# Retention steps of 192 tokens, made a burst early, and one PSUM bank for the second product

## The chip, the cores and the metric

The kernel runs on one core of one Trainium2 chip. The metric is the device time of one execution in microseconds (us), the median of several runs. TensorE (PE in the profile) multiplies, with its weight loads listed as PEld; VectorE is DVE, ScalarE is ACT, GpSimd is POOL, SyncE is SP. An engine works through its own instructions in order, and waits on semaphores for the others.

## The reference

Eight batch entries of 576 tokens, eight heads of 64, go through a retention (an attention with a decay in place of a softmax). The result, 4608 tokens of 512 values, goes through a feed-forward layer with 2048 hidden values.

```python
scores = scale * np.matmul(q, k.transpose(0, 1, 3, 2))
gamma = 1.0 - 2.0 ** (-5.0 - np.arange(H))
Dmat = np.where(rel >= 0, gamma ** rel, 0.0)         # rel = row - column
attn = np.matmul(scores * Dmat, v)                   # then heads side by side: x [4608, 512]
h = x @ w_in                                         # [4608, 2048]
out = (h * (1.0 / (1.0 + np.exp(-1.702 * h)))) @ w_out
```

## The kernel before, in words

**The recorder.** Every operation is recorded with what it reads and writes (`Rec.op`), in the order of the code; the recorder puts it at the end of its engine's queue and adds the semaphore waits. So the order of each engine's work is written out by hand: the order of the calls.

**Retention.** The decay factors into a power on the query side (`gq`, applied when the output leaves PSUM) and one on the value side (`vfac`, applied to v in place by `scale_v`, on VectorE). What is left is a causal product. An entry is cut into five steps of 128, 128, 128, 128 and 64 tokens (`ROWS`); step n is entry n // 5, part n % 5. In a step, scores k q^T go to the bank pair `psS`, VectorE masks them into `sm` (`mask_s`, line 426), and the output is intra (v against the masked scores) plus carried (the state against q). The state, the sum of k^T v over the tokens before, is added up part by part in `zacc` and cast into `zq` (`evac_z`). From entry 1 on everything is made of 64x64 products, which use one quarter of the array each (`scores`, line 404; `values_quarters`, lines 445 intra, 457 state, 464 carried), and k and v of the upper four heads are loaded 64 rows shifted (`load_shifted`). `evac_o` (line 573) multiplies the output by `gq` into `xT`, a buffer for all 4608 tokens.

**Keys and queries turned.** Scores need q and k with the head dimension on partitions. Steps below 10 (`PE_TURNS`, entries 0 and 1) turn them on TensorE (`transposes`, line 366) and copy them with ScalarE (`evac_t`). Later steps use `dma_turn` (line 586): two DMA transposes on SyncE's queue, q of the step and k of the next tile, into one of four buffers `qk`. `burst(n)` asks for the turn of step n + 3.

**Bursts.** `burst(n)` (line 606) holds the products of step n - 1's output and state and, between the two halves of these, the scores of step n. Then VectorE masks step n, evicts step n - 1 and updates the state (`finish`). The second half waits for the first to end (`own=first`). When an entry's last step is finished, `load_entry` asks for the loads three entries on, on POOL's queue (three slots, `NST`).

**Feed-forward.** Nine chunks of 512 tokens. `hidden(c, f)` (line 634) makes 128 of the 2048 hidden values with four matmuls of 512 columns into `psH[0]` or `psH[1]`, and ScalarE writes the activation (line 639). `project(c, r, g)` (line 687) adds a quarter of the second product for 128 tokens, again four matmuls; after g = 3 the bank is copied to `osb` (line 699 VectorE, line 696 ScalarE) and stored by SyncE (line 702). Such a group of four matmuls is called a unit here. From chunk 1's projection on, row blocks alternate between `psU` and `psW` (`pair`).

**Order on TensorE.** Entry 0 alone, chunk 0's products with entry 1's steps between, `hidden_half` of chunk 1 (bursts 8, 9, 10 between), chunk 1's projection (bursts 11 to 13), `hidden` of chunk 2 (bursts 14 to 18), then `region(c)` for chunks 3 to 8. A region alternates the 16 units of chunk c - 1's projection with the 16 of chunk c's first product, in the order O H O H O O H H for each row block, and spreads the bursts that the next chunk needs over its 32 units. Chunk 8's projection ends the kernel.

Of the kernel before, what the change touches and what calls it, by code (L numbers as in the profile page):

```python
# [26 lines left out]
PE_TURNS = 10  # L27
QK_SCALE = 1.0 / math.sqrt(DH)

# [100 lines left out]
def bass_retnet_parallel__then__act_gelu_quick_kernel(  # L130
# [11 lines left out]
    with es:  # L142
# [8 lines left out]
        mask = sb("mask", [P, 2, P], FP32)  # L151
        posj = sb("posj", [P, NC], FP32)
# [9 lines left out]
        gq = sb("gq", [P, NC, HP, 128], FP32)  # L162
# [3 lines left out]
        qk = [sb(f"qk{i}", [P, 2, HP, 128], BF16) for i in range(NQK)]  # L166
        sm = [sb(f"sm{i}", [P, 2, HP, 128], BF16) for i in range(3)]
        zs = sb("zs", [P, HP, 128], BF16)
        xT = sb("xT", [P, HP, B * S], BF16)
# [7 lines left out]
        psS = ps("psS", [P, 2, HP, 128])  # L177
# [36 lines left out]
        def load_entry(b, first=0):  # L214
            if first == 0:
                load(b, 0, "k")
            for c in range(first, NC):
                load(b, c, "q")
                if c + 1 < NC:
                    load(b, c + 1, "k")  # L220
                load(b, c, "v")
# [18 lines left out]
        def constants_first():  # L240
# [22 lines left out]
            for hp in range(HP):  # L263
                R.op("ACT", lambda e, hp=hp: e.activation(
                    gq[:, 0, hp, :], posa.ap(), AF.Exp, scale=lng[:, hp : hp + 1]),
# [7 lines left out]
        def constants_shifted():  # L273
            for r in range(2):
# [3 lines left out]
                    r=["rel"], w=[("mask", 1)])  # L278
            R.op("DVE", lambda e: e.tensor_copy(vfac[1][:, 0:4, :], vfac[0][:, 0:4, :]),
# [14 lines left out]
        def regroup(what):  # L294
# [6 lines left out]
            if what == "gq":  # L301
                t = gT[1][0:64, 8:13, :].bitcast(FP32).rearrange("p c (u n) -> p c u n", u=2)
                swap(gq[0:64, :, 1:4:2, :], gq[64:128, :, 0:4:2, :], t,
# [8 lines left out]
        def later_gq(hp):  # L312
            R.op("ACT", lambda e: e.activation(
                gq[:, 1:NC, hp, :], posi.ap(), AF.Exp, scale=lng[:, hp : hp + 1]),
# [35 lines left out]
        def sides(n):  # L350
# [3 lines left out]
            for a, t, nm, m in ((0, st_q, "q", n), (1, st_k, "k", n if n < NC else n + 1)):  # L354
                if m < NSTEP:
# [15 lines left out]
        def evac_t(n):  # L371
            R.op("ACT", lambda e: e.activation(qk[n % NQK].ap(), psT, AF.Copy),  # L372
# [42 lines left out]
        def mask_s(n):  # L415
            b, c = divmod(n, NC)
            N = ROWS[c]
            if b == 0:
                m = mask[:, 0, 0:N].unsqueeze(1).to_broadcast([P, 2 * HP, N]) if c != 3 else mask3
                o = sm[n % 3].ap().rearrange("p a h c -> p (a h) c")[:, :, 0:N]  # L420
                i = psS.ap().rearrange("p a h c -> p (a h) c")[:, :, 0:N]
            else:
                m = mask[:, :, 0:N].unsqueeze(1).to_broadcast([P, 4, 2, N])
                o = sm[n % 3].ap().rearrange("p a (t u) c -> p (a t) u c", u=2)[:, :, :, 0:N]
                i = psS.ap().rearrange("p a (t u) c -> p (a t) u c", u=2)[:, :, :, 0:N]
# [3 lines left out]
        def values_quarters(n):  # L429
# [46 lines left out]
            if n + 1 < NSTEP:  # L476
                intra(n + 1)
            R.op("PE", part(1), r=r, ps=["O", "Z"], own=first)

# [87 lines left out]
        def evac_o(n, o=None):  # L567
# [3 lines left out]
            t0 = S * b + 128 * c  # L571
            if b > 0:
# [3 lines left out]
                    gq[:, c, :, 0:N].rearrange("p (u j) n -> p u j n", u=2), ALU.mult),  # L576
                    r=[("gq", min(c, 1))], w=[("xT", b, c)], ps=["O", "Z"])
# [381 lines left out]
```

## Time and profile before

| | us |
|---|---|
| three runs | 308.57, 307.38, 306.63 |
| their median | 307.38 |
| the profiled execution, its own time | 306.58 |
| its span, first to last instruction | 304.7 |
| TensorE busy, share of the span | 297.3, 98% |
| ScalarE, VectorE, POOL busy | 108.8, 147.8, 154.2 |
| first product: one matmul of 128x512, modelled | 0.379 |
| mask of 1024 columns (line 426) | 1.223 |
| activation of 512 columns (line 639) | 0.597 |

The profile is of one execution. Its time in the device's account is 1.9 us more than the span that the trace covers. Times inside the trace are counted from the span's start. A busy share is not a rate: matmuls overlap, and a new one of 512 columns starts every 0.216 us although each is shown as 0.379.

### The profile page before, as it was taken

The numbers are of one execution on the slowest core, as the hardware profiler recorded it, in microseconds if no ns is written. First come the engines' busy times: TensorE is split into PE (matmuls) and PEld (weight loads), VectorE is DVE, ScalarE is ACT, GpSimd is POOL, SyncE is SP. The second block draws the span as 40 slices with busy tenths as digits, with TensorE's granted clock in tenths as the row PEclk, the third lists the DMA queues.
The fourth block names the chain that finished last, engine by engine and source line by source line (L and its number), as shares of the span: only waits on it lengthen the run. The fifth ranks groups of instructions, "written<-read, shape, count | busy, mean of one in ns | idle before, by whom it ended". The sixth has DMA issues, their size and how long they took to land.

```text
span 304.7 us, 7234 instructions
## 1 busy us (share of the span) xinstructions
PE 297.3 (98%) x3175; PEld 151.0 (50%) x3175; DVE 147.8 (48%) x246; ACT 108.8 (36%) x183; POOL 154.2 (51%) x208
## 2 busy tenths in 40 slices
PE   7899999999999999999999999999999999999996
PEld 3454545885444444444444444444444444444444
DVE  6689837554767833545546433444364431100012
ACT  8666524661035423322333223323233333333300
POOL 8998999999999999999850000000000000000000
PEclk9999999999999999999999999999999999999999
DMA  9999999999999999999999933213231000001012
GB/s 69 152 195 196 176 168 200 155 145 129 158 194 175 132 156 164 169 161 173 174 169 163 133 84 95 58 38 86 71 80 37 34 37 34 34 37 66 37 54 86
DMA packets 154303, 35.61 MB, mean 117 GB/s; under 512 B 144928, under 2 KB 149792, under 8 KB 154272
## 3 DMA queue, kind: packets, MB, share of 16 engines
q0 software_dynamic: 118384, 18.36, 87.3%
q1 hardware_dynamic: 35888, 16.79, 29.3%
q8 instruction: 25, 0.41, 0.6%
q14 instruction: 6, 0.05, 0.1%
HBM read 36.70 MB, written 9.44 MB: 151 GB/s over the span
## 4 chain that ended last, share of the span: by engine, by line
PE 83%; POOL 9%; DMA 3%; DVE 3%; issue 1%; POOLq 0%
PE psH L634 31%; PE psU L687 18%; PE psW L687 16%; PE psV L445 4%; DMA st_k<-in_k_dram 3%; PE psH L687 3%; PE psH L671 3%; POOL st_k L211 2%; POOL st_q L198 2%; PE psS L404 2%; PE psU L671 1%; PE psV L464 1%; POOL st_k L198 1%; POOL st_v L198 1%; PE psV L457 1%; POOL st_v L211 1%
## 5 line engine op out<-in xcount | busy, mean ns | idle before, releaser
L639 ACT ACTIVATE gT<-psH 128x512 bf16<-128x512 f32 x121 | 72.2, 597 | 153.8 <-PE psH L634 153.8
L634 PE MATMUL psH<-xT,w_in_sb 128*128 128x512 bf16 x484 | 118.1, 379 | 0.0
L426 DVE TENSOR_TENSOR sm<-psS,mask 128x1024 bf16<-128x1024 f32 (+1 forms) x39 | 43.5, 1114 | 85.1 <-PE psS L404 80.8
L634 PEld LDWEIGHTS psH<-xT,w_in_sb 128*128 128x128 bf16 x484 | 45.8, 98 | 54.9 <-ACT gT L639 1.6
L211 POOL DMA_DIRECT2D st_k<-in_k_dram x70 | 69.2, 1250 | 1.6 <-PE psV L464 0.9
L211 POOL DMA_DIRECT2D st_v<-in_v_dram x70 | 68.1, 1240 | 0.0
L687 PE MATMUL psU<-w_out_sb,gT 128*128 128x512 bf16 x256 | 62.7, 379 | 0.0
L687 PE MATMUL psW<-w_out_sb,gT 128*128 128x512 bf16 x224 | 54.8, 379 | 0.0
L198 POOL DMA_DIRECT2D st_q<-in_q_dram x40 | 52.7, 1317 | 0.2 <-issue 0.2
L687 PEld LDWEIGHTS psU<-w_out_sb,gT 128*128 128x128 bf16 x256 | 24.2, 98 | 28.0
L687 PEld LDWEIGHTS psW<-w_out_sb,gT 128*128 128x128 bf16 x224 | 21.3, 98 | 25.0
L343 DVE TENSOR_TENSOR st_v<-st_v,vfac 128x512 bf16<-128x512 bf16 x37 | 25.2, 680 | 3.1 <-DMA st_v<-in_v_dram 3.1
L699 DVE COPY osb<-psU 128x512 f32<-128x512 f32 x15 | 10.3, 687 | 28.6 <-PE psU L687 28.6
L573 DVE TENSOR_TENSOR xT<-psV,gq 128x512 bf16<-128x512 f32 (+1 forms) x35 | 21.9, 627 | 4.2 <-PE psV L464 4.2
L699 DVE COPY osb<-psW 128x512 f32<-128x512 f32 x14 | 9.6, 689 | 21.7 <-PE psW L687 21.7
L687 PE MATMUL psH<-w_out_sb,gT 128*128 128x512 bf16 x80 | 18.7, 379 | 0.0
L445 PE MATMUL psV<-sm,st_v 64*64 64x64 bf16 (+1 forms) x504 | 17.5, 214 | 0.3
L445 PEld LDWEIGHTS psV<-sm,st_v 64*64 64x64 bf16 x504 | 9.1, 104 | 15.7 <-issue 12.1
L372 ACT ACTIVATE qk<-psW 128x1024 bf16<-128x1024 bf16 x10 | 10.2, 1023 | 9.2 <-PE psW L366 9.2
L457 PE MATMUL psV<-st_v,st_k 64*64 64x64 bf16 x448 | 13.0, 192 | 0.0
L464 PE MATMUL psV<-qk,zq 64*64 64x128 bf16 (+1 forms) x224 | 12.6, 215 | 0.1
L687 PEld LDWEIGHTS psH<-w_out_sb,gT 128*128 128x128 bf16 x80 | 7.6, 98 | 8.5
(108 smaller groups left out, 212.7 us busy)
## 6 DMA issues: line engine op xcount, KB each, us to landing
out_dram<-osb SPq DMA_DIRECT2D x35, 256.0 KB, 2.4
st_q<-in_q_dram POOLq DMA_DIRECT2D x32, 128.0 KB, 17.5
st_k<-in_k_dram POOLq DMA_DIRECT2D x57, 64.0 KB, 17.2
st_v<-in_v_dram POOLq DMA_DIRECT2D x57, 64.0 KB, 17.2
w_out_sb<-in_moe_w_out_dram POOLq DMA_DIRECT2D x4, 512.0 KB, 11.9
w_in_sb<-in_moe_w_in_dram POOLq DMA_DIRECT2D x3, 512.0 KB, 7.8
st_k<-in_k_dram POOLq DMA_DIRECT2D x4, 128.0 KB, 4.2
st_v<-in_v_dram POOLq DMA_DIRECT2D x4, 128.0 KB, 4.6
```

The lines of the kernel that those rows point to most:

```text
L198: R.op("POOL", lambda e, d=d, s=s: e.dma_start(d, s), w=[(nm, sl, c)], dma=(nm, sl, c))
L211: R.op("POOL", lambda e: [e.dma_start(d, s) for d, s in parts], w=[(nm, sl, c)], dma=(nm, sl, c), parts=2)
L343: R.op(eng, lambda e: e.tensor_tensor(t, t, f, ALU.mult), r=[("vfac", min(b, 1))], w=[("v", sl, c)])
L426: R.op("DVE", lambda e: e.tensor_tensor(o, i, m, ALU.mult), r=[("mask", 0), ("mask", 1)] if b else mask3_keys if c == 3 else [("mask", 0)] ...
L445: i = e.matmul(psV[half(t), u, 128 * j + 64 * last : 128 * j + N], st_v[rows, sl, cc, 64 * h : 64 * h + 64], s[rows, j, 2 * t + u, 64 * la ...
L457: i = e.matmul(psV[half(j), u, 256 + 64 * t : 320 + 64 * t], st_k[rows, sl, cc, hs], st_v[rows, sl, cc, hs], start=False, stop=False, skip ...
L464: i = e.matmul(psV[half(t), u, 128 * j : 128 * j + N], zq[(c - 1) % 2][half(j), 2 * u + t, :], qk[n % NQK][half(j), 0, 2 * u + t, 0:N], st ...
L573: R.op("DVE", lambda e: e.tensor_tensor(xT[:, :, t0 : t0 + N].rearrange("p (u j) n -> p u j n", u=2), psV[:, :, 0:256].rearrange("p u (j n ...
L634: i = e.matmul(bank.ap(), w_in_sb[:, a, 128 * f : 128 * f + 128], xT[:, a, 512 * c : 512 * c + 512], start=(a == 0), stop=(a == 3))
L639: R.op("ACT", lambda e: e.activation(gT[c % 2][:, f, :], bank.ap(), AF.Gelu_apprx_sigmoid), w=[("gT", c % 2, f)], ps=[key])
L687: i = e.matmul(bank, gT[c % 2][:, f, 128 * r : 128 * r + 128], w_out_sb[:, f, :], start=(f == 0), stop=(f == NF - 1))
L699: R.op("DVE", lambda e: e.tensor_copy(osb[m].ap(), bank), w=[("osb", m)], ps=[key])
```

## The change

From entry 2 on an entry is done in three steps of 192 tokens, each of three 64-token blocks (`WIDE`, `NB`); step s is entry s // 3, part s % 3, so they run from 6 to 23. Every block has its own state ahead of it, so scores are only needed within a block (64 by 64, mask `mask64`). `prepare(s)` makes the scores of step s and the state products of its blocks, `states(s)` adds those up on VectorE in `zf` and casts them into `zw`, and both are called in the burst of step s - 1. `wide_burst(s)` holds the outputs of step s in two parts, with `prepare(s + 1)` between. The lists of products are interleaved so that four in a row use four quarters (`quads`). `dma_turn(s)` turns whole tiles of 128 tokens of both k and q into a buffer for two entries, and `wide_burst(s)` calls it for step s + 2. State products use `psW`, so the second product of the regions keeps to `psU` and is copied by ScalarE. `xT` becomes a ring of 1536 columns. The loads of entries 2 on are asked for in another order. Entries 0 and 1 keep their steps.

```diff
-PE_TURNS = 10
+XR = 1536
+WIDE = 192
+NB = WIDE // 64
+FIRST_WIDE = 6
+LAST_WIDE = B * S // WIDE - 1
...
+            if b >= 2:
+                for c, what in ((0, "kq"), (1, "kq"), (0, "v"), (1, "v"), (2, "kq"), (3, "k"),
+                                (2, "v"), (3, "v"), (3, "q"), (4, "kqv")):
+                    for one in what:
+                        load(b, c, one)
+                return
...
+                R.op("DVE", lambda e, rows=rows: e.tensor_copy(mask64[rows, :], mask[rows, 0, rows]),
...
-                if m < NSTEP:
+                if m < 2 * NC:
...
+        def tiles(s):
+            return ((0, 1), (2, 3), (4,))[s % NB]
+        def q_tiles(s):
+            return [("qT", s // NB % 2, m) for m in ((0, 1), (1, 2), (3, 4))[s % NB]]
+        def k_tiles(s):
+            return [("kT", s // NB % 2, m) for m in ((0, 1), (1, 2, 3), (3, 4))[s % NB]]
...
+        def dma_turn(s):
...
+            for m in tiles(s):
+                for a, t, nm in ((1, st_k, "k"), (0, st_q, "q")):
+                    rows = P if nm == "k" else ROWS[m]
+                    R.op("SP", lambda e, a=a, t=t, rows=rows, m=m: e.dma_start_transpose(
+                        out=qkT[:, buf, a, :, 128 * m : 128 * m + rows], in_=t[0:rows, sl, m, :]),
+                        r=[(nm, sl, m)], w=[(nm + "T", buf, m)] + olds, dma=("turn", buf, a, m))
...
+        def outputs(s, part):
+            c = s % NB
+            out = {}
+            for r in range(2):
+                u = (r + c + part) % 2
+                for t in range(2):
+                    todo = []
+                    for m in ((0, 2), (1,))[part]:
...
+                        for j in range(2):
+                            h = 4 * u + 2 * t + j
+                            todo.append((psV[half(t), u, WIDE * j + 64 * m : WIDE * j + 64 * m + 64],
+                                         st_v[half(r), sl, slot, 64 * h : 64 * h + 64],
+                                         smw[s % 2][half(r), j, 64 * (2 * m + t) : 64 * (2 * m + t) + 64],
+                                         adds if todo or part else starts))
+                    for m in range(1 if c == 0 else 0, NB):
+                        i = NB * c + m
+                        todo.append((psV[half(t), u, WIDE * r + 64 * m : WIDE * r + 64 * m + 64],
+                                     zw[half(r), s % 2, m, 2 * u + t, :],
+                                     qkT[half(r), s // NB % 2, 0, 2 * u + t, 64 * i : 64 * i + 64],
+                                     adds))
+                    out[r, t] = todo
+            return out
...
+        def prepare(s, turn):
+            c = s % NB
+            kv = kv_keys(s, "k") + kv_keys(s, "v")
+            done = R.op("PE", products(quads(joined(state_part(s, 1, 0, turn),
+                                                    state_part(s, 1, 1, turn)))),
+                        r=kv, ps=["O", "Z", "W"])
+            todo = [state_part(s, 0, 0, turn), state_part(s, 0, 1, turn), wide_scores(s)]
+            if c < 2:
+                todo.insert(0, state_part(s, 2, 0, turn))
+            R.op("PE", products(quads(joined(*todo))),
+                 r=kv + q_tiles(s) + k_tiles(s), ps=["S", "W"])
+            R.op("DVE", lambda e: e.tensor_tensor(
...
+                mask64.ap().unsqueeze(1).unsqueeze(1).to_broadcast([P, 2, 6, 64]), ALU.mult),
+                r=["mask64"], w=[("sm", s % 2)], ps=["S"])
+            return done
...
+        def states(s, turn):
+            c = s % NB
+            for m in range(NB if c < 2 else 2):
...
+                for r in range(2):
...
+                        R.op("DVE", lambda e, o=o, a=a, new=new: e.tensor_tensor(o, a, new, ALU.add),
...
+            R.op("DVE", lambda e: e.tensor_copy(zw[:, s % 2, 1:NB], zf[:, 1:NB]),
...
+            if c < 2:
+                R.op("DVE", lambda e: e.tensor_copy(zw[:, (s + 1) % 2, 0], zf[:, 0]),
...
+        def wide_burst(s):
+            more = s < LAST_WIDE
+            if more:
+                scale_tiles(s + 1)
...
+            first = done = R.op("PE", products(quads(outputs(s, 0))), r=r, ps=["O", "Z"])
+            second = outputs(s, 1)
+            if more:
+                done = prepare(s + 1, s % NB)
+                second = joined(second, last_state(s + 1, s % NB))
+            R.op("PE", products(quads({x: second[x][:2] for x in second if x[0] == 1})),
+                 r=r, ps=["O", "Z"], own=first)
+            R.op("PE", products(quads({x: second[x][2 * x[0] :] for x in second})),
+                 r=r, ps=["O", "Z"], own=done)
+            if s + 2 <= LAST_WIDE:
+                dma_turn(s + 2)
+            wide_evac(s)
+            if more:
+                states(s + 1, s % NB)
+            b = s // NB + NST
+            if s % NB == 2 and b < B:
+                load_entry(b)
...
         def burst(n):
...
+            if n == 2 * NC:
+                scale_tiles(FIRST_WIDE)
+            values_quarters(n - 1)
...
-        pair = [wide[0], (psW.ap(), "W")]
-        between = {0: 11, 5: 12, 10: 13}
+        between = {5: 6, 11: 7}
         for i in range(16):
-            project(1, i // 4, i % 4, *pair[i // 4 % 2])
+            project(1, i // 4, i % 4, *wide[(1, 0)[i // 4 % 2]], eng="ACT")
             if i in between:
-                burst(between[i])
-        between = {0: 14, 3: 15, 7: 16, 10: 17, 13: 18}
+                wide_burst(between[i])
+        between = {1: 8, 8: 9, 14: 10}
...
+        def last_wide(c):
+            return (512 * (c + 1) - 1) // WIDE
...
-                    project(u[1], u[2], u[3], *pair[u[2] % 2])
+                    project(u[1], u[2], u[3], *wide[0], eng="ACT")
                 if i in at:
-                    burst(at[i])
+                    wide_burst(at[i])
```

Between the two, `burst(10)` holds step 9's output and `prepare(6)`, `burst(9)` calls `dma_turn(6)` and `burst(10)` calls `dma_turn(7)`. In region 3 the wide bursts 11, 12 and 13 stand behind units 5, 15 and 25; where a region has two, behind 7 and 22.

## The prediction

> **What bounds the kernel now.** I read the page first: who is busy, when the DMA engines are, and whose chain ends last.
>
> ```profile
> PE 297.3 (98%) x3175; PEld 151.0 (50%) x3175; DVE 147.8 (48%) x246; ACT 108.8 (36%) x183; POOL 154.2 (51%) x208
> ...
> DMA  9999999999999999999999933213231000001012
> ...
> PE 83%; POOL 9%; DMA 3%; DVE 3%; issue 1%; POOLq 0%
> ```
>
> TensorE has no slack from about 45 us on, so a burst's own length counts in full, and so does any wait put in front of it. The DMA row is the second thing to see: its engines are full for the first 23 of 40 slices, to about 175 us, although TensorE hardly waits for them. Next, TensorE's timeline through one burst (start, duration, then the group):
>
> ```profile
> 107.72 0.31 PE L445 MATMUL psV<-sm,st_v 64*64 64x128 bf16 x8
> 107.86 0.23 PE L457 MATMUL psV<-st_v,st_k 64*64 64x64 bf16 x8
> 107.92 0.23 PE L464 MATMUL psV<-qk,zq 64*64 64x128 bf16 x4
> 107.97 0.23 PE L404 MATMUL psS<-qk 64*64 64x64 bf16 x8
> 108.22 0.26 PE L445 MATMUL psV<-sm,st_v 64*64 64x64 bf16 x8
> ...
> 108.53 1.04 PE L687 MATMUL psU<-w_out_sb,gT 128*128 128x512 bf16 x4
> ```
>
> Read the starts. Eight 64x64 state products go by in 0.06 us: they run four at once, one on each quarter of the array, so a round of four with 64 columns takes 0.03; the round with 128 columns (107.92 to 107.97) takes 0.05. The burst lasts 107.72 to 108.53, 0.81 us. The chain of waits (start, duration) shows the cost behind it:
>
> ```profile
> 121.41 0.86 PE psU L687 x4
> ...
> 122.97 0.97 PE psH L634 x4
> ```
>
> Four feed-forward matmuls take 0.97 us right after a burst and 0.86 elsewhere: some 0.10 more, so 0.91 per burst. Last, SyncE's timeline, and the landing times of the DMA transposes in 81.5 to 91 us and then in 178 to 225 us:
>
> ```profile
> 76.58 1.28 SPq L586 DMA_TRANSPOSE qk<-st_q  x1
> 77.90 1.96 SPq L586 DMA_TRANSPOSE qk<-st_k  x1
> 79.90 0.59 SPq L702 DMA_DIRECT2D out_dram<-osb  x1
> 81.81 1.25 SPq L586 DMA_TRANSPOSE qk<-st_q  x1
> 83.11 1.30 SPq L586 DMA_TRANSPOSE qk<-st_k  x1
> ```
> ```profile
> DMA to landing us min/median/max: 6.8/7.0/8.3
> ```
> ```profile
> DMA to landing us min/median/max: 2.4/2.5/3.6
> ```
>
> SyncE issues one transpose in 1.3 us and it lands 7 to 8 us later while loads fill the DMA engines, 2.5 us later once they have stopped. Today a transpose is issued three bursts ahead of its scores, so none of this is on the path.
>
> **Bursts get fewer (gain).** An entry costs today five bursts. From their starts and the 0.10 behind each: 0.80 (first, no carried state), three of 0.91, 0.62 (last, no new state): 4.15 us. The rounds inside a full one are 6 of 0.053 and 8 of 0.031, 0.57; the other 0.34 is entry, exit and a wait for its own first half. The first and last leave 0.34 and 0.33 by the same count, so it is a price per burst. The new code issues 272 products of 64 columns per entry (72 scores, 72 intra, 64 carried, 64 states) where the old had 240, 88 of them with 128 columns. Laid on four quarters as the lists interleave them, some rounds half full, I count 24, 24 and 26 rounds: 74 x 0.031 = 2.29, plus 3 x 0.31 (I drop 0.03 of the wait, since more rounds now lie between the halves) = 3.22. Gain 0.93 per entry, 5.6 over entries 2 to 7. Bounds: 0.34 per burst gives 5.0; 0.28 and no half rounds 7.2. Turn 9 on TensorE loses its key half, 0.2 us (55.60 to 55.83). Gain together 5.8.
>
> **Transposes come one burst ahead instead of three (loss).** Per entry there are still ten, 1.3 us of SyncE each. But step s+2 is now asked for at the end of burst s, and its scores sit inside burst s+1. SyncE's queue runs in order, with the output stores in it, so a store that waits for its projection holds the transposes behind it. Spacings on TensorE: a unit (four matmuls) 0.864, a wide burst about 1.05.
> - Step 6: four transposes, from 54.3 (chunk 0's last projection ends at 52.7, copy and store take 0.6 each) to 58.25. The pairs issued at 58.1 and 59.4 landed after 9.3 and 9.1 us: 67.35. Scores could start at 65.6: 1.7 us of wait.
> - Step 7: key tile 3 issued by 64.5, landed by 75 even at the longest landing, 10.6; needed at 77.0. Nothing.
> - Step 8: two, behind the store of row block 0 of chunk 1 (its last unit ends at 75.2, copy 0.6, store 0.5): 76.5 and 77.8, landing after 7.7 (the four between 73 and 80 us): 85.5. Burst 7 comes six units after burst 6, at 83.0; scores at 83.3. Wait 2.2.
> - Step 9: recorded behind the store of row block 2, which ends exactly where burst 7 stands. Store at 84.0; four transposes at 84.5, 85.8, 87.1, 88.4, the last landing after 7 to 8.3 us, say 7.7: 96.1. Burst 8 stands six units behind burst 7, scores at 91.6. Wait 4.5 (3.8 to 5.1). Steps 8 and 9 share this: less wait in one is more in the other.
> - Steps 10 to 12: about 101.5, 105.5 and 112 against 103, 109 and 117. Nothing.
> - Step 13: behind the store of region 3's first row block, issued at that very burst (11). Key tile 3 goes third, 4.1 us after the burst's start, and lands 7.2 later; scores 10 units on, 10.0 us after that start. Wait 1.3.
> - From step 14 on the distance is 8.6 to 13 us, and from 175 us a landing takes 2.5. Nothing.
>
> Sum 9.7. Ends: 6 with a landing of 6.7 (the shortest before 170 us) throughout, 13 with 9.3. I take the rows nearest in time.
>
> **VectorE.** Behind each burst: mask and eviction of 768 columns (from 0.69 at 512 and 1.22 at 1024: 0.95 each), six state sums of 128 columns (0.41 at 256, 0.68 at 512, so 0.28 each), the cast of two blocks (0.38 for 256 columns, so 0.7) and of the third (0.38), one or two scalings of 0.68: 5.3 to 6.0 us. Six units take 5.3, seven 6.1. The next burst's outputs need the cast, its state products the scaling. I take 0.5 us of wait in the two short intervals that no transpose wait covers (9 to 10, 8 to 9); the ends are 0 and 2.8, the latter if a cast of 256 columns takes the 0.73 seen at 97 us (two such, 0.35 more each, in four intervals). Over an entry VectorE does less than before: 16.6 us by these prices against 18.0 (masks 5.6, evictions 3.1, states 2.8, scalings 3.4, output copies 3.1), since the copies leave it.
>
> **One bank for the second product.** In the regions the copy of psU moves to ScalarE (0.6 us). It must end before the next row block's first unit; two first-product units, 1.73 us, lie between. Cost nothing. Without that cover each of 24 copies would cost some 0.7. ScalarE is busy 36%.
>
> **Rest.** The load order inside an entry changes, not its bytes: POOL's queue and the landing of an entry as a whole stay, and the transposes above already wait longer for SyncE than for loads, and the values of a tile land within 8 us of its keys, ahead of their scaling. A slot that is freed later (entry 7 waits for burst 14) holds POOL a few us, some 70 us ahead of use. Two 64-column copies for the mask at the start (between 0.06 and 0.29 each, by the 1- and 128-column rows) delay POOL at 24 us, where loads already queue 9 us: nothing, at most 0.6. The ring of 1536 columns makes no wait: the chunk it overwrites has been read a region earlier.
>
> Sum: 306.6 - 5.8 + 9.7 + 0.5 = 311.0 us. That is off the profiled execution, which lies 0.8 below the median of the runs; off the median it would be 311.8. I keep 311.0.
>
> **Rivals.**
> - *The transposes are there in time: faster.* It decides where the waits fall below the gain of 5.8, at a landing near 6.3 us; 2.5 us, as after 175, leaves 1.3 for step 9 and gives 306.6 - 5.8 + 1.3 + 0.5 = 302.6. For it: with fewer stores between, transposes might pass quicker. Against: no landing before 170 us is under 6.7, and loads are unchanged. 0.20.
> - *The long wait cools TensorE.* The first eleven fill matmuls take 4.35 us, 0.40 each where a warm one takes 0.216. If the 4.5 us wait brings that back, it costs 11 x 0.18 = 2.0: 313.0. The trace has no wait that long once TensorE is warm, so it can't say. The Trainium skill (TensorE: Matmul & The Clock Gate, "Part 1: The HAM clock gate") says that an idle window of about 3.4 us halves the clock, and that the window runs free; by it the stretch after step 9 would run at half rate. 0.13.
> - *Products cost by number, not by round.* 4.15 us over 240 is 17.3 ns; 272 cost 4.70, a loss of 3.3 instead of a gain of 5.6: 319.9. Against: eight in 0.06. 0.08.
> - The Trainium skill (TensorEngine Tiling (Array Packing), "Instruction Overhead") gives every matmul some 60 cycles; an estimate of 25 ns each in sequence would make an entry's 272 take 6.8 us. The row of eight in 0.06 us disagrees, as long as four quarters share the time.
> - *VectorE paces the early bursts*: the 2.8 above, 313.3. 0.07.
>
> **Chances.** My forecast 0.52 (its own range 307 to 315). 1%, about what a measurement here tells from no change, is 304.3 to 310.4. Faster: the first rival, 0.20. Within: 0.23, the lower part of my range and the rest of that rival's. Slower: 0.57, the upper part and the other three. The range 301.5 to 317 leaves out the price by number and little else.
>
> **What would show it.** Right: wide bursts near 1.05 us where nothing waits; TensorE's scores waiting for DMA landings in bursts 10, 7, 8 and 12 and nowhere after 135 us; burst 8's the longest. Wrong: landings well under 7 us before 170, stores that do not hold transposes, a burst of 1.4 us, or waits on VectorE's casts instead.

## The result and the profile after

| | us |
|---|---|
| kernel before, median of 4 runs beside it | 307.0 (306.5 to 308.6) |
| changed kernel, median of 4 runs | 337.2 (336.8 to 339.5) |
| ratio, with its 95% interval | 1.099 (1.092 to 1.105) |
| profiled execution: its time, its span | 339.5, 337.7 |

The change made the kernel 10% slower, where 1.4% was forecast and 317 us was the upper end of the range. Medians here are over all runs of a kernel, ratios over its undisturbed runs alone, so the two can differ a little.

The page of the changed kernel shows that TensorE, 98% busy before, now stands still for a tenth of the span:

```profile
PE 302.5 (90%) x3363; PEld 152.4 (45%) x3363; DVE 131.1 (39%) x280; ACT 125.0 (37%) x211; POOL 154.7 (46%) x208
...
PE   7899999869670569799999999999999999999996
...
DMA  9999999999999999899999842640452001000012
...
PE 66%; DMA 20%; POOL 6%; DVE 3%; SPq 1%; ACT 1%; issue 1%; POOLq 0%
```

Each digit is a fortieth of the span, 8.4 us. The damage lies between slices 8 and 17, some 65 to 143 us; behind it TensorE is busy again without a break. The last line is the chain that ended last: a fifth of the span now hangs on DMA, 3% before. The DMA engines are as full in that stretch as before (all but one of its digits are 9), yet from 65 to 145 us they move 131 GB/s where the kernel before moves 161. So no more is asked of them than before, and what TensorE waits for must be late for another reason. The table by stage (window, its length, then the busy time of TensorE, its weight loads, VectorE, ScalarE and POOL with instructions, the granted clock, the DMA share and GB/s) shows what the waits bring with them, a clock that is no longer granted in full. The DMA share adds up the time that packets took; they overlap, so it can pass 1:

```profile
45.00:65.00 20.00, 19.33 (x341) 14.19 (x339) 14.33 (x21) 11.04 (x17) 20.00 (x29) 1.00 2.07 170
65.00:95.00 30.00, 23.27 (x340) 13.21 (x339) 12.50 (x31) 5.55 (x10) 30.00 (x42) 0.89 2.33 154
95.00:119.00 24.00, 9.33 (x124) 4.24 (x122) 5.44 (x13) 2.92 (x5) 21.95 (x30) 0.64 2.20 145
119.00:145.00 26.00, 19.86 (x240) 8.62 (x239) 9.54 (x22) 7.82 (x14) 13.78 (x20) 0.80 1.23 92
145.00:330.00 185.00, 184.92 (x1931) 87.83 (x1930) 55.72 (x129) 71.05 (x119) 25.98 (x35) 1.00 0.59 76
```

The granted clock is 1.00 from 45 to 65 us and again from 145 us on, and 0.64 about the longest wait. The waits (total, times, longest) name the transposes:

```profile
PE psW L670 <- DMA qkT<-st_q: 17.4, 2, 14.7
PE psS L670 <- DMA qkT<-st_q: 5.0, 2, 2.8
PE psW L670 <- DMA qkT<-st_k: 4.0, 1, 4.0
...
PE psV L492 <- DVE sm L757: 1.1, 1, 1.1
```

TensorE's timeline has them in bursts 10, 7, 8, 9 and 10 of the wide steps (the first "10" is the last narrow burst, at 66 us). The longest stands in the middle of wide burst 8:

```profile
98.73 0.32 PE L670 MATMUL psV<-sm,st_v 64*64 64x64 bf16 x16
...
99.01 0.20 PE L670 MATMUL psV<-st_v,st_k 64*64 64x64 bf16 x2
113.88 0.26 PE L670 MATMUL psW<-st_v,st_k 64*64 64x64 bf16 x2 [14.67 <-DMA qkT<-st_q]
```

Sixteen outputs, the carried products and the first state products of step 9 go by in 0.3 us; then the operation that holds the scores waits 14.67 us for one transpose. SyncE's timeline says why it came so late. These are step 9's and 10's transposes, entry 3's first:

```profile
88.91 1.23 SPq L647 DMA_TRANSPOSE qkT<-st_k  x1
96.93 1.19 SPq L647 DMA_TRANSPOSE qkT<-st_q  x1
103.72 1.19 SPq L647 DMA_TRANSPOSE qkT<-st_k  x1
109.29 1.19 SPq L647 DMA_TRANSPOSE qkT<-st_q  x1
110.54 0.57 SPq L932 DMA_DIRECT2D out_dram<-osb  x1
113.81 1.20 SPq L647 DMA_TRANSPOSE qkT<-st_k  x1
118.48 1.19 SPq L647 DMA_TRANSPOSE qkT<-st_q  x1
```

Each takes 1.2 us of SyncE, yet they start 8.0, 6.8, 5.6, 4.5 and 4.7 us apart: each is issued when the one before has landed (the first landed at 96.85, the second at 103.66, the third at 109.23, the fourth, for which TensorE waits, at 113.75). The cause is a line of the change that the diff above leaves out:

```python
olds = [("qk", i, a) for i in range(NQK) for a in range(2)] if b == 3 else []
...
        r=[(nm, sl, m)], w=[(nm + "T", buf, m)] + olds, dma=("turn", buf, a, m))
```

The four small buffers of entries 0 and 1 now lie inside the second half of `qkT`, which entry 3 is the first to fill. A key such as `("qk", i, a)` is the name under which the recorder knows a piece of memory. By this list every one of entry 3's ten transposes is recorded as writing all four old buffers, and the recorder lets a writer of a key wait for the writer before it. Ten transposes that touch ten different places stand in one line.

**The account.** From the starts on TensorE, a wait is the length of a burst less that of one in which nothing waits (0.74, 0.91 and 1.07 us). Bursts 10, 7, 8, 9 and 10: 4.2 + 3.2 + 15.0 + 4.4 + 2.3 = 29.1 us. The clock was halved five times, for 3.4 us or more. Eight matmuls in 3.4 us, one per 0.43 us instead of 0.216, lose 1.7; the five stretches together lose 9.1. Entry 1's first transposes on TensorE started 0.9 later, waiting for loads. Shorter bursts give 5.9 back: 29.1 + 9.1 + 0.9 - 5.9 = 33.2, and the spans are 33.0 apart.

### The profile page after: what moved, and what is told of

It reads as the page before. It is cut to its first block, busy times and chain, and to the rows that moved or that the text cites. A ratio compares the mean times of both kernels' runs of the same rounds, so it can differ in the third digit from the quotient of the medians.

```text
span 337.7 us, 7671 instructions
## 1 busy us (share of the span) xinstructions
PE 302.5 (90%) x3363; PEld 152.4 (45%) x3363; DVE 131.1 (39%) x280; ACT 125.0 (37%) x211; POOL 154.7 (46%) x208
## 4 chain that ended last, share of the span: by engine, by line
PE 66%; DMA 20%; POOL 6%; DVE 3%; SPq 1%; ACT 1%; issue 1%; POOLq 0%
PE psU L917 27%; PE psH L865 25%; DMA qkT<-st_q 9%; DMA qkT<-st_k 8%; PE psH L917 4%; DMA st_k<-in_k_dram 3%; POOL st_k L228 2%; PE psV L670 2%; POOL st_v L228 2%; PE psH L978 2%; PE psS L670 1%; SPq L647 1%; PE psH L901 1%; POOL st_q L215 1%; ACT qkT L400 1%
## 5 line engine op out<-in xcount | busy, mean ns | idle before, releaser
L917 PE MATMUL psU<-w_out_sb,gT 128*128 128x512 bf16 x448 | 112.3, 386 | 0.0
L757 DVE TENSOR_TENSOR sm<-psS,mask 128x768 bf16<-128x768 f32 x18 | 17.2, 958 | 128.9 <-PE psS L670 124.1
L917 PEld LDWEIGHTS psU<-w_out_sb,gT 128*128 128x128 bf16 x448 | 43.5, 99 | 52.4 <-issue 3.3
L926 ACT ACTIVATE osb<-psU 128x512 f32<-128x512 f32 x27 | 16.1, 597 | 39.6 <-PE psU L917 39.6
L795 DVE TENSOR_TENSOR xT<-psV,gq 128x768 bf16<-128x768 f32 x18 | 17.1, 949 | 10.8 <-PE psV L670 10.8
L917 PEld LDWEIGHTS psH<-w_out_sb,gT 128*128 128x128 bf16 x112 | 10.6, 98 | 12.2
L929 DVE COPY osb<-psU 128x512 f32<-128x512 f32 x1 | 0.7, 691 | 38.0 <-PE psU L917 38.0
L454 DVE TENSOR_TENSOR sm<-psS,mask 128x1024 bf16<-128x1024 f32 (+1 forms) x9 | 10.0, 1107 | 10.9 <-PE psS L432 5.7
L400 ACT ACTIVATE qkT<-psW 128x1024 bf16<-128x1024 bf16 x9 | 9.2, 1022 | 9.8 <-PE psW L390 9.8
L901 PE MATMUL psH<-xT,w_in_sb 128*128 128x256 bf16 x88 | 11.8, 286 | 0.0
L670 PE MATMUL psV<-sm,st_v 64*64 64x64 bf16 x432 | 10.9, 199 | 0.1
```

Of the source, the lines that this page charges most:

```text
L400: R.op("ACT", lambda e: e.activation(qk[n % NQK], psT, AF.Copy), w=[("qk", n % NQK, 0), ("qk", n % NQK, 1)], ps=["W"])
L670: i = e.matmul(o, w, m, **kw)
L757: R.op("DVE", lambda e: e.tensor_tensor(smw[s % 2].rearrange("p j (m n) -> p j m n", n=64), psSw[:, :, 0:384].rearrange("p j (m n) -> p j ...
L795: R.op("DVE", lambda e: e.tensor_tensor(xT[:, :, x0 : x0 + WIDE].rearrange("p (u j) n -> p u j n", u=2), psV[:, :, 0:384].rearrange("p u ( ...
L901: m = e.matmul(bank[:, 256 * i : 256 * i + 256], w_in_sb[:, a, 128 * (f + i) : 128 * (f + i) + 128], xT[:, a, a0 : a0 + 256], start=(a == ...
L917: i = e.matmul(bank, gT[c % 2][:, f, 128 * r : 128 * r + 128], w_out_sb[:, f, :], start=(f == 0), stop=(f == NF - 1))
```

## The experiments

x1 to x4, x5 to x8, x9 to x12, and x13 with x14 each ran on one chip, beside the kernel before. x4, x9 and x14 change the kernel before, x7 and x11 add to x4; the others start from the changed kernel.

### The chain, the distance, the spacing, the bank

**x1_olds_once**: only the first transpose of entry 3 writes the old buffers; the others follow it on the same queue.

```diff
-            olds = [...] if b == 3 else []
+            olds = [...] if s == 3 * NB else []
...
                         r=[(nm, sl, m)], w=[(nm + "T", buf, m)] + olds, dma=("turn", buf, a, m))
+                    olds = []
```

> The changed kernel, with the old buffers named as written by the first transpose of entry 3 alone instead of by all ten. Theory A (each of entry 3's transposes waits for the one before it to land, only because all ten are recorded as writing the same old buffers): TensorE's waits in bursts 9 and 10 (4.1 and 2.4 us) go, the one in burst 8 falls from 14.9 to 4 or 5, and the half clock behind bursts 9 and 10 goes with them; 337.2 - 10.4 - 6.5 - 4 = about 316 us. Rival B (the transposes are slow because the DMA engines are full, and the list of old buffers costs nothing): within 2 us of 337.

Measured: 319.0 us (318.6 to 320.7), ratio 1.036 (1.031 to 1.042). SyncE's timeline of x1 at the same place:

```profile
88.34 1.23 SPq L647 DMA_TRANSPOSE qkT<-st_k  x1
89.61 1.38 SPq L647 DMA_TRANSPOSE qkT<-st_q  x1
91.04 1.38 SPq L647 DMA_TRANSPOSE qkT<-st_k  x1
92.47 2.54 SPq L647 DMA_TRANSPOSE qkT<-st_q  x1
```

They now start 1.3 to 1.4 us apart, and burst 8 waits 3.7 us (by starts) instead of 14.9. One list in one line cost 18 of the 30 us. What is left: bursts 10, 7, 8, 10 and 12 are 14.9 us too long together, and half clock costs 5.2 us. Of the 14.9, 12.2 are what the prediction had described, waits for transposes in bursts 10, 7, 8 and 12. The narrow burst 10 has 1.1 us of waiting for a mask besides. The wide burst 10 has a stop of 1.6 us that is no wait for a transpose; x2 has the same stop, and x11 tells what it is.

**x2_three_ahead**: x1, with the transposes asked for three bursts ahead.

```diff
-            if s + 2 <= LAST_WIDE:
-                dma_turn(s + 2)
+            if s + 3 <= LAST_WIDE:
+                dma_turn(s + 3)
...
+            if n == 2 * NC:
+                dma_turn(FIRST_WIDE + 2)
```

> The run before it, and burst s asks for the turn of step s + 3 instead of s + 2 (burst 10 for steps 7 and 8). Theory A: the waits of bursts 7 and 8 go too, and what is left is burst 10's wait of 2.9, its 1.3 for the mask and 1.7 of half clock; 307.0 - 5.8 + 4.2 + 1.7 + 0.5 = 307.6 us. Rival C (more transposes in flight land later, so the waits come back): landings over 10 us between 75 and 110 us and a time over 312.

Measured: 310.8 us (308.2 to 314.4), ratio 1.010 (1.007 to 1.013). The distance was worth 8 us. The time lies 3 us above theory A's and under theory C's. After the narrow burst 10 no wait for a transpose is left, but TensorE stops in bursts 7 to 11, in the middle of operations, 5.0 us together. Its timeline, three of the five stops:

```profile
87.71 0.22 PE L671 MATMUL psS<-st_v,st_k 64*64 64x64 bf16 x2
88.81 0.25 PE L671 MATMUL psS<-st_v,st_k 64*64 64x64 bf16 x6 [0.88 <-issue]
...
103.10 0.26 PE L671 MATMUL psS<-qkT 64*64 64x64 bf16 x9
103.80 0.28 PE L671 MATMUL psS<-qkT 64*64 64x64 bf16 x11 [0.44 <-issue]
...
110.10 0.20 PE L671 MATMUL psV<-sm,st_v 64*64 64x64 bf16 x2
111.85 0.22 PE L671 MATMUL psV<-sm,st_v 64*64 64x64 bf16 x4 [1.56 <-issue]
```

An operation's semaphore wait stands before its first product. Here an operation has begun, goes on for a few products and stops, and the releaser is "issue": nothing that the profile shows. I took these at first for late loads, and x5 was made under that belief.

**x3_later_and_free**: x2, with burst 10 four units later and without a wait for VectorE's mask, which exists only because step 9's second half is recorded as reading a buffer that the mask of step 6 writes.

```diff
-            R.op("PE", part(1), r=r, ps=["O", "Z"], own=first)
+            R.op("PE", part(1), r=r[1:], ps=["O", "Z"], own=done)
...
-        between = {1: 8, 5: 9, 11: 10}
+        between = {1: 8, 5: 9, 15: 10}
```

> The run before it, with burst 10 four units later (behind the last half unit of chunk 1's first product) and the second half of step 9's products no longer recorded as reading the mask buffer, which it does not read. Theory A: no wait over 0.5 us on a transpose anywhere and no half clock after the start; 307.0 - 5.8 + 0.5 = 301.7 us, between 301 and 303. Rival D (bursts gain nothing net, the products' number counts): 307 or more.

Measured: 309.0 us (306.1 to 313.1), ratio 1.004 (1.001 to 1.008); theory A missed. Burst 10 now waits for nothing. But the bursts behind it come 5 to 6 us earlier than in x2 and find other things late: a stop of 1.2 us in burst 7, waits of 2.0, 1.1 and 3.0 in bursts 8, 9 and 10 for transposes, and 2.6 us of half clock behind the last. SyncE's queue shows late loads: it issued three transposes, at 84.9, 87.2 and 96.2 us, within 0.03 us of the landing of the loads that they read, and the ones that bursts 9 and 10 wait for stand behind these. The losses are 9.9 us, the gain of the bursts is 5.9; the difference is 4.0, and the spans are 3.8 apart.

**x4_before_one_bank**: the kernel before, with the second product of the regions in `psU` alone and copied by ScalarE.

```diff
-                    project(u[1], u[2], u[3], *pair[u[2] % 2])
+                    project(u[1], u[2], u[3], *wide[0], eng="ACT")
```

> The kernel before, with the second product of the regions in psU alone and copied by ScalarE: one part of the change by itself. The prediction's step (two units of 0.86 us cover the copy): 307 us, within 1. Rival (each row block waits for the copy): 24 copies of 0.7 us, 324 us; half of that if one unit covers it.

Measured: 306.8 us (306.4 to 308.0), ratio 0.999 (0.996 to 1.001). One bank costs nothing, as the prediction had it.

### Room between the bursts, and the price of a wait

**x5_spread**: x3, with the whole of chunk 2's projection ahead of chunk 3's hidden layer, so that bursts 8 to 13 can stand 8 to 10.5 us apart.

```diff
-        between = {1: 8, 8: 9, 14: 10}
+        between = {2: 8, 12: 9}
...
+        between = {5: 10, 14: 11}
+        for i in range(16):
+            project(2, i // 4, i % 4, *wide[(1, 0)[i // 4 % 2]], eng="ACT")
...
+        between = {6: 12, 14: 13}
+        for f in range(NF):
+            hidden(3, f)
...
-        for c in range(3, NCH):
+        for c in range(4, NCH):
```

> As x3, with the wide bursts 8 to 13 spread: the whole projection of chunk 2 is put ahead of the hidden layer of chunk 3, so that bursts 8 to 13 lie 8 to 9.5 us apart instead of 5.3 us. Theory A (what x3 still lost, waits of 1.2 + 2.0 + 1.1 + 3.0 us in bursts 8 to 11 and 2.6 us of half clock behind the last, comes from the bursts being closer together than the loads and transposes of the entries can follow): the waits go but for 1 us in all, no half clock, and the burst gain of 5.9 us is left: 301 us (300 to 303). Theory B (the transposes come late whatever the spacing, because each queue is served in order and lands them 8 to 9 us after the issue): the same waits at later places, 306 us or more.

(The bursts of x3's losses are numbered one too high there; they are 7 to 10.) Measured: 302.8 us (301.9 to 303.1), ratio 0.984 (0.981 to 0.987). No stretch of half clock. Two stops are left, 1.5 us in burst 7, in the middle of an operation as in x2, and 0.65 in burst 8, a wait for a transpose. Room between the bursts was what x3 lacked, and the change now pays.

**x6_spread_two_ahead**: x5, with the transposes asked for as in the changed kernel.

```diff
-            if s + 3 <= LAST_WIDE:
-                dma_turn(s + 3)
+            if s + 2 <= LAST_WIDE:
+                dma_turn(s + 2)
...
-            if n == 2 * NC:
-                dma_turn(FIRST_WIDE + 2)
```

> As x5, but the transposes asked for where the changed kernel asks for them, one burst ahead of their use. Theory A (with room between the bursts the distance no longer matters): 301 to 302 us, as x5. Theory C (one burst ahead is too late even so: a step with two tiles has four transposes, some 1.35 us apart on SyncE's queue, the last landing about 8.5 + 3 x 1.35 = 12.5 us after the first is issued, against 9 to 9.5 us to its use): waits of about 3 us in bursts 7, 8, 9 and 11, with half clock behind some: 308 to 315 us.

Measured: 313.9 us (312.3 to 315.3), ratio 1.021 (1.018 to 1.025). Theory C: waits of 2.5, 2.5 and 4.1 us in bursts 7, 8 and 11, two of them followed by half clock. Even with bursts 8 us and more apart, one burst ahead is too late: it costs 11 us.

**x7_pauses**: the kernel of x4 with pauses in its last regions, in which VectorE copies a bank that TensorE must write next. It turned out to hold 18 of them, 0.95 to 3.07 us long by TensorE's starts, 37.4 us together.

```diff
...
+            R.op("PE", touch, r=["idle"], ps=["W"])
+            left, k = int((us - 0.35) / 0.69 * 512), 0
+            while left > 0:
+                n = min(left, 512)
+                R.op("DVE", lambda e, n=n, k=k: e.tensor_copy(scratch[:, k, 0:n], psW[:, 0:n]),
+                     w=[("scratch", k)], ps=["W"])
+                left, k = left - n, k + 1
+            R.op("PE", touch, r=["idle"], ps=["W"])
```

> The kernel before with one bank for the second product, and 17 pauses in its last regions: VectorE copies a bank for 1.0 to 3.4 us while TensorE has to wait for it. It computes the same; the pauses add 38 us by their lengths. Theory A (a wait of about 2.3 us or more is followed by 3.4 us of half clock, 1.7 us lost each): eight pauses of 2.4 us or more, 306.8 + 38 + 13.6 = 358 us. Theory B (a wait costs its length and no more, the half clock came from something else in those stretches): 306.8 + 38 = 345 us, and the granted clock stays at 1.0 through the pauses.

Measured: 353.7 us (2 runs). The pauses in the view of waits, and the table by stage about two of them, which end at 186.8 and 206.7 us (the granted clock is the third number from the right):

```profile
PE psW L879 <- DVE scratch L885: 33.9, 18, 2.9
```
```profile
175.00:187.00 12.00, 8.57 (x87) 3.94 (x86) 5.52 (x10) 3.82 (x7) 0.00 (x0) 1.00 0.31 78
187.00:190.40 3.40, 3.40 (x10) 1.21 (x8) 0.35 (x1) 0.02 (x1) 0.00 (x0) 0.50 0.00 0
190.40:207.40 17.00, 13.36 (x138) 6.37 (x139) 8.32 (x14) 5.35 (x9) 0.00 (x0) 1.00 0.24 59
207.40:210.90 3.50, 3.50 (x10) 1.26 (x9) 0.00 (x0) 0.60 (x1) 0.00 (x0) 0.51 0.00 0
```

Full clock, 3.4 us of half clock right behind a pause, full clock again. The nine pauses up to 2.01 us have none behind them; of the nine from 2.17 us on, five do (2.17, 2.38, 2.69 and both of 3.07) and four do not (2.39, 2.54 twice, 2.69). 307.4 + 37.4 + 5 x 1.7 = 353.3. The result lies between the theories, nearer to A: here a wait costs its length up to 2 us, and from there on 1.7 us more about every second time. Length alone doesn't decide it: x14 below has a wait of 3.4 us, at 103.2 to 106.7 us of its trace, with the clock granted in full all through.

**x8_busy_waits**: x1, with idle products in bursts 10, 7 and 8 ahead of the ones that wait.

```diff
...
+            if s in (6, 8, 9):
+                busy({6: 8, 8: 12, 9: 14}[s])
```

> As x1, with 8, 12 and 14 idle products of 0.216 us put into bursts 10, 7 and 8 ahead of the products that wait there, so that TensorE works for most of a wait that it has anyway (it computes the same). Theory A (the waits bring the half clock): the stretches of half clock behind bursts 7 and 8 go, 2.8 us of the 5.2 us that x1 lost so, 316 us; behind burst 10 the second wait, for the mask, may keep its own. Theory B (half clock has another cause): 319 us or, with the idle products partly on the path, 320 us.

Measured: 317.7 us (313.8 to 318.9), ratio 1.029 (1.024 to 1.035), beside 1.036 (1.031 to 1.042) for x1. The half clock behind bursts 10, 7 and 8 is gone, so the waits bring it. The time gained is less than forecast and the intervals overlap: TensorE came sooner to the next bursts and lost time there, 1.8 us by a stop in the wide burst 10 and 3.1 by a wait in burst 12, with a stretch of half clock behind it.

### Code that comes late, and the order of the loads

**x9_before_load_order**: the kernel before with the change's order of loads.

```diff
         def load_entry(b, first=0):
+            if b >= 2:
+                for c, what in ((0, "kq"), (1, "kq"), (0, "v"), (1, "v"), (2, "kq"), (3, "k"),
+                                (2, "v"), (3, "v"), (3, "q"), (4, "kqv")):
+                    for one in what:
+                        load(b, c, one)
+                return
```

> The kernel before with the order of loads of the change for entries 2 on, and nothing else. Theory A (the order of the loads plays no part, as the prediction had it): 307 us, ratio 0.995 to 1.005. Theory D (the new order brings the values of the early steps too late): waits of VectorE for st_v and 309 us or more.

Measured: 312.6 us over 4 runs that lie from 306.6 to 314.4, ratio 1.005 (0.998 to 1.013). Its profile has two waits for transposed keys, 2.7 us together, and one stretch of half clock. That leaves open whether the order costs anything, so x14 repeats it.

**x10_spread_more**: x5 with bursts 7 to 10 one or two units later.

```diff
-        between = {5: 6, 11: 7}
+        between = {5: 6, 12: 7}
-        between = {2: 8, 12: 9}
+        between = {4: 8, 13: 9}
-        between = {5: 10, 14: 11}
+        between = {6: 10, 14: 11}
```

> As x5, with bursts 7, 8, 9 and 10 moved 1, 2, 1 and 1 units of 0.86 us later. In x5 TensorE stood for 1.5 us in burst 7 and 0.65 us in burst 8. The stop in burst 7 is in the middle of one operation, with nothing to wait for, at a place that is a whole number of blocks of 256 TensorE instructions from the stops of x2. Theory F (TensorE has run out of code: a block of 256 instructions takes about 8 us to follow the one before while the DMA engines are full): burst 7 comes 0.86 us later against the block's landing, its stop falls to 0.6 us, burst 8's goes: 301.3 us (300.5 to 302). Theory N (these are waits for loads): the loads of step 8 were landed by 81.2 us and the stop would be the same length: 302.8 us.

Measured: 302.1 us (301.4 to 303.1), ratio 0.983 (0.980 to 0.986). The stop in the middle of burst 7's operation is gone, and so is burst 8's wait, so theory N misses. Theory F wanted 0.6 us of that stop left; the 0.36 us that burst 7 still loses stand ahead of an operation and end with the landing of a transpose, at 83.80 us. The time is 0.8 us above F's forecast. The only wait of a wide burst that x10's list of waits still has is that one:

```profile
PE psS L671 <- DMA qkT<-st_q: 0.2, 1, 0.2
```

**x11_tiny_products**: the kernel of x4 and two lots of 384 idle products of 64 by 64, one where the DMA engines are full and one where they are nearly idle.

```diff
...
+            if f == 5:
+                small_lot(384)
...
+                if c == NCH - 1 and i == 10:
+                    small_lot(384)
```

> The kernel before with one bank for the second product, and two lots of 384 idle products of 64 by 64 in 64 columns (768 TensorE instructions each, three blocks of 256): one in the middle of the hidden layer of chunk 2, at about 90 us, where the DMA engines are full, and one in the last region, at about 265 us, where they are nearly idle. It computes the same. Theory F (code comes by blocks of 256 instructions, some 7.5 to 8 us each while the DMA engines are full): the first lot has two or three stops 256 instructions apart and takes 16 us or more; the second has shorter stops, 2 to 4 us each. Theory N (code is no limit): each lot takes about 3 us (384 products at 31 ns for four), the whole 313 us.

Measured: 335.7 us (2 runs). TensorE's timeline at the stops:

```profile
97.79 0.19 PE L596 MATMUL psS<-idle 64*64 64x64 bf16 x1 [3.53 <-issue]
...
105.08 0.21 PE L596 MATMUL psS<-idle 64*64 64x64 bf16 x1 [5.98 <-issue]
...
112.10 1.13 PE L646 MATMUL psH<-xT,w_in_sb 128*128 128x512 bf16 x3 [3.75 <-issue]
...
296.90 0.21 PE L596 MATMUL psS<-idle 64*64 64x64 bf16 x1 [2.02 <-issue]
...
300.63 0.39 PE L646 MATMUL psH<-xT,w_in_sb 128*128 128x512 bf16 x1 [1.76 <-issue]
```

Idle products read no data that could be late, and they stop all the same. From stop to stop it is 7.3 and 7.0 us in the first lot, and 3.7 us in the second. A product and its weight load are two records in TensorE's list. Counted so, and with TensorE's semaphore instructions, these stops lie 256 records apart (some 255, since a few records are missing). So do x2's: its five stand at records 1984, 2240, 2496, 2752 and 3008, and x1's stop in the wide burst 10 at 2752. The first lot took 13.9 us, the second 5.4. The queue that the profile calls "instruction" moved one 16 KB packet shortly ahead of each stop's end: in x2 at 86.3 us for the stop that ended at 88.8, and at 93.7 for the next, at 96.0. For all five of x2's stops the packet's end lies 1.2 to 1.7 us before TensorE goes on. Theory F: TensorE had no code.

**x12_shifted_code**: x2 with 20 idle products at the start.

```diff
...
         fill(14)
+        small_lot(20)
```

> As x2, with 20 idle products of 64 columns (40 TensorE instructions) put in at the start, while TensorE has nothing to do. Theory F (x2's stops of 1.1, 0.8, 0.6, 1.8 and 0.7 us in bursts 7 to 11 are ends of blocks of code): each stop comes 20 products earlier in the work, in another kind of product: in burst 7 among the first group's products with the old state, not among the new state's. Theory N (they are waits for data): the stops stay at the same products. The time is x2's, 310 to 311 us, by both.

TensorE's timeline of x12 in bursts 9 and 10:

```profile
98.50 0.21 PE L671 MATMUL psS<-st_v,st_k 64*64 64x64 bf16 x1
98.87 0.19 PE L671 MATMUL psS<-st_v,st_k 64*64 64x64 bf16 x1 [0.16 <-issue]
...
105.13 0.24 PE L671 MATMUL psS<-qkT 64*64 64x64 bf16 x6
105.83 0.34 PE L671 MATMUL psS<-qkT 64*64 64x64 bf16 x18 [0.45 <-issue]
```

In x2 these bursts stopped behind their 55th and 70th product, here behind the 35th and the 50th: 20 earlier to the product, in other kinds of product. So the place of these two stops belongs to the code, not to the data; the other three can't say. Those of bursts 7 and 11 were absent, and burst 8 had only 0.4 us that the profile puts down to a transpose. The time missed: 306.5 us (305.4 and 307.6), under x2's. The two stops were shorter (0.37 and 0.65 us against 0.64 and 1.75), the clock never fell, and the narrow burst 10 waited 1.0 us instead of 2.0. Two runs on another chip don't say how much of that is the shift.

**x13_old_load_order**: x10 with the loads in the order of before, so with x9's lines taken out. **x14_before_load_order_again**: the kernel of x9 in more rounds.

> As x10, with the loads of entries 2 on in the order of the kernel before (keys one tile ahead, then queries and values tile by tile). Theory A (the order plays no part once the transposes are asked for three bursts ahead): 302.1 us, ratio 0.98 to 0.987. Theory D (the new order is needed by wide steps, whose scores want two tiles of keys and queries at once): waits for transposes in bursts 7 to 9 and 304 us or more.

> The kernel of x9 once more in more rounds. Theory A (the order of the loads plays no part in the kernel before): ratio 0.997 to 1.003. Theory D (the waits of 0.9 and 2.3 us for transposed keys that x9's profile shows in two bursts, with 1.7 us of half clock, come with the new order in most runs): 309 to 313 us, ratio above 1.006.

Measured: x13 302.0 us (300.6 to 302.9), ratio 0.982 (0.980 to 0.985), the same as x10. x14 308.4 us over 12 runs (306.3 to 312.7), ratio 1.002 (1.000 to 1.005). Its median is 1.5 us above that of the kernel before beside it (306.9), and four of its runs lie above 310 us where none of the 17 of the kernel before is above 308.6. So the new order costs the kernel before little or nothing in most executions and 2 to 6 us in some; x14's profile, of such a one, has 3.8 us of waits for turned keys. In the changed kernel, with transposes asked for early enough, the times show no difference.

## Why the prediction was wrong

**The gain of the bursts: right.** An entry was to cost 3.22 us. Where nothing waits, wide bursts last 0.91, 0.91 and 1.07, with 0.10 behind each 3.19. TensorE's timeline of the changed kernel through burst 6, first and last row:

```profile
81.61 0.32 PE L670 MATMUL psV<-sm,st_v 64*64 64x64 bf16 x16
...
82.52 1.90 PE L917 MATMUL psU<-w_out_sb,gT 128*128 128x512 bf16 x8
```

The account closes with 5.9 us of gain in the changed kernel, x1, x2 and x3. Products cost by rounds of four on four quarters, and the rival "by number" is out, as long as TensorE has its code.

**The transposes: the step that failed.** The prediction saw that they are asked for too late, and where: waits in bursts 10, 7 and 8, the longest in burst 8. Its terms for steps 6 and 8, 1.7 and 2.2, measured 2.7 and 2.8 by the waits view (with TensorE at burst 10 0.6 later than assumed). Step 9 was "at 84.5, 85.8, 87.1, 88.4, the last landing after 7 to 8.3 us": 4.5 us of wait, measured 14.7. Steps 10 to 12 were "Nothing"; steps 10 and 11 measured 4.0 and 2.2. Both go wrong at one place: the issues were put 1.3 us apart, which is what SyncE needs for one, and they came 4.5 to 8 us apart, which is what one needs to land. The line with `olds` was part of the change. It had to be read as the recorder reads it: ten writers of the same keys. x1 takes away nothing else and gives 18 us back. With x1 the forecast's own mechanism stays: 12.2 us of waits for transposes, more than its 9.7 and within its ends of 6 and 13. Even so x1 takes 319.0 us, above the range; without its 5.2 us of half clock it would lie inside.

**Step 13's 1.3** didn't occur in the changed kernel, where the bursts before it came late; in x1 burst 12 waits 2.6.

**The clock: a rival that came true and was priced too low.** It had 2.0 us and a chance of 0.13, for one wait of 4.5 us, and was taken as excluding the forecast, though it only adds to it. It cost 9.1 us in five places, behind waits of 2.4 us and more, and 5.2 us in x1. The Trainium skill (TensorE: Matmul & The Clock Gate, "Part 1: The HAM clock gate") speaks of an idle window of about 3.4 us that runs free. The stretches of 3.4 us and their multiples agree with a window; x7 adds that pauses of 2.2 to 3.1 us, shorter than it, already brought one in five of nine cases.

**VectorE: small, as forecast, but elsewhere.** 0.5 us was set for its casts and scalings. TensorE waits 1.1 us for it once, in burst 10, for a mask that the recorder believes step 9 to read. No wide burst waits for it.

**One bank: right** (x4). **The order of the loads: "Nothing"** holds for the changed kernel (x13), and for most runs of the kernel before (x14).

**The cover that nobody priced.** A burst earlier means all loads, transposes and code a burst earlier too. In the changed kernel the long waits hid this; x2 and x3 show it as soon as they are gone. A burst has 176 or 192 instructions of TensorE and lasts about 1 us; the 5.3 us of feed-forward between two bursts have 48. So 256 instructions, a block of code, are used up in about 7 us, just what a block takes there.

What is settled by runs: the chain (18 us, x1), the distance of one burst (8 us in x2, 11 in x6), the spacing (6 us, x5), each with the half clock it brings. How much of the spacing's 6 us is code and how much late transposes isn't separated by a run; x3's profile has 1.2 us of code, 6.1 of transposes and 2.6 of half clock. x5 also moves chunk 2's projection as a whole, and no run has that order without the room; that the room is the cause rests on the waits that are gone.

## What to carry to other kernels

When a buffer takes over the place of old ones, give the hand-over to the first writer alone: a key that every writer carries turns independent DMAs into a chain, and its price is a landing time each, not an issue time each. When work is moved earlier on a queue-ordered engine, ask for its transfers by landing time plus the issue of all transfers of a step, and leave room between dense bursts, since data and code both come at a pace. A wait of over 2 us on TensorE can cost more than its length. With the hand-over, the distance and the room mended, and the needless wait for a mask taken out (x10: 302.1 us, against 307.4 for the kernel before), the same change turns from 10% slower into 1.7% faster.

## What the runs showed of the hardware

- TensorE's code arrives in blocks of 256 instructions. While the DMA engines are full a block follows the last after 7.0 to 8.1 us (x11, x2), and after 3.7 us while they are nearly idle. A lot of 768 instructions took 13.9 us in the first case and 5.4 in the second. The Trainium skill (Runtime: NRT & Kernel Launch, "Instruction fetch mechanics") has the blocks of 256 instructions and their own DMA queue, and calls the crossing mostly hidden. The runs agree on the size. In them the crossing is hidden only while 256 instructions last longer than those times.
- A granted clock of one half comes in stretches of 3.4 us or multiples. In x7 five of the nine pauses from 2.17 us on brought one, and none of the nine up to 2.01 us. A wait of 3.4 us in x14 brought none, so length alone doesn't decide.
- Landing times of DMA transposes, as the chain of the changed kernel shows them one by one: 7.9 us for the one issued at 88.9 us, then 6.7 and 5.5 (from 95 to 119 us the DMA engines move 145 GB/s), 4.1 to 4.6 for the six issued from 109 to 132 us, and 2.3 for the last, at 135.9 (92 GB/s from 119 to 145 us).
